# Chunked scan and two MoE layers on one core: fewer filler products, another order of weight-conversion steps before MoE1, and one scan request a chunk sooner

## The chip, the cores and the metric

The kernel runs on one core of a Trainium2 chip. The metric is device time in microseconds (us) of one execution. The five engines are named as in the profile: PE (TensorE, with PEld for its weight loads), DVE (VectorE), ACT (ScalarE), POOL (GpSimd) and SP (SyncE, which here only issues DMAs; the profile writes SPq for it).

## What is computed

A chunked state-space scan feeds two dense layers. Shortened from the reference:

```
# x [4,8,768,32], a [4,8,768], B and C [4,8,768,16]
la  = log(clip(a, 1e-6, 1));  cum = cumsum(la) inside a chunk
L   = exp(cum_i - cum_j), causal
y   = ((C B^T) * L) x  +  (C state) * exp(cum)
state = exp(sum la) * state + sum_j B_j x_j exp(cum_last - cum_j)
# y becomes x [3072, 256]
MoE1: h = x @ w_in;  g = max(h,0) + alpha*min(h,0);  x = g @ w_out     # d_ff 2048
MoE2: x = (sigmoid(x @ w_gate) * (x @ w_val)) @ w_out2                 # d_ff 1536
```

## The kernel before, in words

**Scan.** The four sequences of 768 positions are cut into 32 chunks of 96, eight to a sequence. A chunk c passes through four stages, each a function of its own. `ev_decay` (L367) multiplies the operands dl and dr into d on PE and has ACT take exp of it (L399), which gives lt. `ev_scores` (L403) multiplies B and C (tiles bt and ct) into cb on PE (L424). `ev_weigh` (L440) has DVE multiply cb by lt into mt (L448) and, for the first chunks, form bd (L459). `ev_out` (L461) multiplies on PE into yd (L472, L478), after which ACT copies the state to the next chunk's xs (L489) and the result to x1 (L491, or L484 for chunk 5). From chunk 7 on d has a single bank of PSUM, so the product of chunk c+1 waits until ACT's exp of chunk c has read it; cb has one bank from the start, so the scores of chunk c+1 wait for mt of chunk c.

**The loop (L1034).** Iteration i issues mt of chunk i (for early i), d of chunk i+1, yd of chunk i-1 and cb of chunk i+1, in that order on PE. For i below `lead` = 7 nothing else is there for PE, and `keep_busy` (L904) issues filler products of a constant tile (nobody<-heat, 128x512 bf16), whose result nobody reads: one at i = 0, three at i = 1 and 2, two at i = 3 to 6. From i = 7 on, one MoE1 step runs in each iteration: `moe1_in` (L520) multiplies the first 512 positions by a block of w_in into h, ACT forms t (L534), DVE forms g (L538), `halves` splits g into gh (ACT, L562) and gl (DVE, L563), and one iteration later `moe1_out` (L576) multiplies both by w_out into acc (L586). Before that, the finished chunks are split into xh (ACT L516, DVE L518), in three pieces.

**Weight conversion.** The weights come as 64-bit numbers. POOL requests them in tiles raw of 512 KB (L148), and `work` (L164) turns each into a high part and a low part in seven steps: 0 scale (ACT L160), 1 shift (DVE L190 or two of L193), 2 copy of the group before (L177: on POOL while i < 7, then on ACT), 3 clip (DVE L198), 4 low part of the group before (L179: on POOL while i < 7, then on DVE), 5 combine (DVE L202; for the first groups it also scales the next one on ACT), 6 combine (DVE L207). `feed(n, ...)` (L216) issues the next n steps. How many are issued in an iteration is `now` (L1078): EARLY = 4 for i = 1 to 6, then FIRST = 5 for the first eight MoE1 steps, then LATER = 4.

**Requests.** In each iteration SP requests dl and dr of chunk i+3 (`load_cum`, L322), xs of chunk i+3 (`load_x`, L278) and, once per four chunks, the bt and ct of a whole chunk group (`load_bc`, L292: one transfer of 192 KB for bt, four of 48 KB for ct, after dl, dr and xs of the same iteration). SP's transfers use eight counters in turn. A transfer is issued only when the one eight places ahead of it in SP's order, which has the same counter, has landed. Which chunk group is requested when is set by `soon` (L1072): the third group (chunks 8 to 11) at i = 5.

All engines work through their instructions in the order in which the program issues them, so the order of the calls in the loop is the order of the queues.

Of the kernel before, what the change touches and what calls it, by code (L numbers as in the profile page):

```python
# [37 lines left out]
AT_CHUNK = {1: 3, 4: 4, 5: 5, 6: 6, 7: 7}  # L38


EARLY = 4
FIRST = 5
LATER = 4

NX = 6
# [7 lines left out]
def kernel(  # L53
# [100 lines left out]
    def scale(g):  # L154

        if g < len(queue) and g not in mags:
            mags[g] = ring.tile([128, 2, WG], F32, tag="mag", name="mag", bufs=3)
            nc.scalar.activation(  # L160
                mags[g], raws[g][:, :, :, 1].bitcast(F32), AF.Copy, scale=2.0 ** -112
            )
# [53 lines left out]
    def feed(n, groups):  # L216

        for _ in range(n):
            if worked[0] < ready(groups - 1):
                work()  # L220
# [8 lines left out]
    first2 = len(queue)  # L229
# [18 lines left out]
    ZC = ZG * G  # L248
# [73 lines left out]
    def load_cum(c):  # L322
        b, k = divmod(c, CPB)
        s = slice(k * T, (k + 1) * T)
        if c < CPB - 1:

            rows = bf(parts[0:2 * H, s])
            for l in range(2):
                nc.sync.dma_start(out=bf(dr[c % NC][W + l:W + l + 1]), in_=rows[l:2 * H:2])
            nc.sync.dma_start(out=bf(dl[c % NC][T:W, 0:T]), in_=rows)  # L330
            return
        nc.sync.dma_start(
            out=bf(dl[c % NC][T:W, 0:T]), in_=cum_d[b].rearrange("h l s -> (h l) s")[:, s]
        )
        nc.sync.dma_start(
            out=bf(dr[c % NC][W:KD]), in_=cum_d[b, :, :, s].rearrange("h l t -> l h t")
        )
# [23 lines left out]
    lead = -(-BL // T) + 1  # L361
# [78 lines left out]
    def ev_weigh(c):  # L440
        MT[c] = m = aring.tile([W, H, T], F32, tag="mt", name="mt", bufs=3)
        last = ahead_of_this(nc.vector)
        if c >= ZC:
            split = lambda t: t.rearrange("j (q e) t -> j q (e t)", e=2)
            nc.vector.tensor_tensor(split(m), CBT.pop(c), split(LT[c]), op=ALU.mult)
        else:
            split = "j (e q) t -> j e q t" if c < ND else "j (q e) t -> j e q t"
            nc.vector.tensor_tensor(  # L448
                m.rearrange(split, e=2),
                CBT.pop(c)[:, :, 0:4 * T].rearrange("j e (q t) -> j e q t", t=T),  # L450
                LT[c].rearrange(split, e=2), op=ALU.mult,
            )
        if c % CPB < CPB - 1:
            BD[c] = bd = aring.tile([W, H, N], F32, tag="bd", name="bd", bufs=3)
            args = (bd, b_of(c), LT[c][:, :, T - 1:T].broadcast_to([W, H, N]))
            if c >= lead:
                behind(nc.gpsimd.tensor_tensor(*args, op=ALU.mult), last)
            else:
                nc.vector.tensor_tensor(*args, op=ALU.mult)  # L459
# [42 lines left out]
    def setup_flip():  # L502
        nc.vector.tensor_scalar(
            flip, sign.bitcast(U32), 0x80000000, None, op0=ALU.bitwise_and
        )
# [3 lines left out]
    def split_x(kind, k, lo=0, hi=BL, which="hl"):  # L509

        if lo == 0:
            xh[kind, k] = ring.tile([128, 2, KT, BL], F32R, tag="xs", name="xh", bufs=2)
        t = xh[kind, k][:, :, :, lo:hi]
        src = x1[:, :, k * BL + lo:k * BL + hi]
        if "h" in which:
            nc.scalar.copy(t[:, 0], src)  # L516
        if "l" in which:
            nc.vector.tensor_tensor(t[:, 1], src, bf(t[:, 0]), op=ALU.subtract)  # L518
# [50 lines left out]
    half = NF1 // 2  # L569
# [309 lines left out]
    with tc.manual_schedule():  # L879
# [24 lines left out]
        def keep_busy(n):  # L904
            p = psum.tile([128, 512], F32, tag="h", name="nobody")
            for _ in range(n):
                nc.tensor.matmul(p, heat[:, 0:128], heat, start=True, stop=True)  # L907
# [15 lines left out]
        def copy_eye(i):  # L923
            nc.gpsimd.tensor_copy(
                xs[i][T:W, H * D:].rearrange("s (h n) -> s h n", n=N),
                eye_c.unsqueeze(1).broadcast_to([N, H, N]),
            )
# [62 lines left out]
        def setup_left(j):  # L990

            nc.scalar.copy(dl[j][0:T], left_c)
            nc.scalar.copy(dl[j][T:KD], rows_c)

        def setup_right(j):
            (nc.vector.tensor_copy if j < 2 else nc.scalar.copy)(dr[j][0:W], bf(early_r))

        def follow(c):

            t = bf(dr[2]) if c == 0 else (MT if c == 1 else LT)[c]  # L1000
            nc.gpsimd.tensor_copy(scrap, t[0:1, 0, 0:1])
# [21 lines left out]
        def later_cum():  # L1023
            halve_cum(pieces[2], nc.scalar)
            for j in (2, 3):
                copy_eye(j)
            setup_alpha()
            store_cum()
# [4 lines left out]
        at = 0  # L1033
        for i in range(NCH + 1):  # L1034
            go = i >= lead
            early[0] = not go
            if i < min(NCH, ZC):
                ev_weigh(i)

            if i == lead // 2 + 1:  # L1040
                split_x("m1", 0, 0, BL // 2)
            if i == lead - 1:
                split_x("m1", 0, BL // 2, (lead - 2) * T)
            if i == 0:
                later_cum()
            if i == 1:
                setup_left(1)
                load_cum(4)
                scale(0)
                for j in range(2):  # L1050
                    setup_right(j)
                keep_busy(2)
            if i == lead:
                for h in range(2):
                    nc.gpsimd.dma_start(
                        out=units_z[h:128:2],
                        in_=k_misc[64 * h:64 * h + 64, 0:N].rearrange("(n k) c -> k n c", k=NP),
                    )
            if i in AT_CHUNK:
                follow(i)  # L1060
                ahead[0] = AT_CHUNK[i]
                take_up()
            if i == 1:
                for j in range(4, NX):
                    copy_eye(j)
            if i == 2:
                setup_flip()
            if 1 < i < NCH - 3:
                load_cum(i + 3)
            if 1 < i < NCH - 3:  # L1070
                load_x(i + 3)
            soon = i + 3 + (i + 4 >= ZC)  # L1072
            if G < soon < NCH and soon % G == 0:
                load_bc(soon)
            if i == NCH:
                open_banks()
            over = at > 1 and ends[steps[at - 2][1:]][1]
            now = 0 if i == 0 else EARLY if not go else FIRST if at < half else LATER  # L1078
            if i >= ZC:
                high_half(steps[at - 1])  # L1080
                if over:
                    moe1_done(steps[at - 2][1], alone=True)
                    now = 1
                elif at - 1 in (half + 1, 2 * half + 1):
                    now = 5
                if i + 1 < NCH:
                    ev_decay(i + 1)
                feed(now, first2)
                now = 0
                low_half(steps[at - 1])  # L1090
            else:
                if at > 0:
                    halves(steps[at - 1])
                if over:
                    moe1_done(steps[at - 2][1])
                ev_decay(i + 1)
                if go:
                    feed(now // 2, first2)
                    now -= now // 2

            def chunk():
                if i + 1 == ZC:
                    open_banks()
                if i + 1 < NCH:
                    ev_scores(i + 1)
                ev_out(i - 1)
                if i + 1 < NCH:
                    ev_weigh(i + 1)

            if go:  # L1110
                step_in(at, "h", later=chunk if i + 1 >= ZC else None)
            if i + 1 < ZC:
                if i > 0:
                    ev_out(i - 1)
                ev_scores(i + 1)
            if not go:
                keep_busy(1 if i == 0 else 3 if i < 3 else 2)
            if go:
                if at > 0:
                    step_out(at - 1, two=False)  # L1120
                splits(at)
                at += 1
            if i == lead - 1:
                feed(1, first2)
                split_x("m1", 0, (lead - 2) * T, BL, "l")
                now -= 1
            feed(now, first2)

            if i in (10, 12):
                lo = (i - 10) * BL // 4  # L1130
                split_x("m1", 1, lo, lo + BL // 2)
# [132 lines left out]
```

## Time and profile before

| | before |
|---|---|
| median of 3 runs | 626.7 us (626.63 to 629.47) |
| the profiled execution | 627.08 us |
| its span | 625.2 us |
| PE busy | 618.9 us, 99% |
| DVE busy | 515.3 us, 82% |
| ACT busy | 364.5 us, 58% |
| POOL busy | 73.8 us, 12% |
| chain of work that ended last | PE 97%, ACT 1%, DVE 1% |

Busy time of PE is to be read with care: its products are pipelined and their ends are modelled. All times in the rows are us from the start of the span unless ns is written. The first 29 us are the scan alone, up to the first product of MoE1; from there to about 140 us scan and MoE1 run side by side; then come the rest of MoE1 and MoE2.

### The profile page before, as it was taken

The numbers are of one execution on the slowest core, as the hardware profiler recorded it, in microseconds if no ns is written. First come the engines' busy times: TensorE is split into PE (matmuls) and PEld (weight loads), VectorE is DVE, ScalarE is ACT, GpSimd is POOL, SyncE is SP. The second block draws the span as 40 slices with busy tenths as digits, with TensorE's granted clock in tenths as the row PEclk, the third lists the DMA queues.
The fourth block names the chain that finished last, engine by engine and source line by source line (L and its number), as shares of the span: only waits on it lengthen the run. The fifth ranks groups of instructions, "written<-read, shape, count | busy, mean of one in ns | idle before, by whom it ended". The sixth has DMA issues, their size and how long they took to land.

```text
span 625.2 us, 11455 instructions
## 1 busy us (share of the span) xinstructions
PE 618.9 (99%) x4430; PEld 519.2 (83%) x4430; DVE 515.3 (82%) x883; ACT 364.5 (58%) x725; POOL 73.8 (12%) x110
## 2 busy tenths in 40 slices
PE   9999999999999999999999999999999999999997
PEld 4466777778888888888888889999999999999996
DVE  7999988867878778787676988888888888888876
ACT  7988788875656665665565444544544544544443
POOL 9845211100000000000000000000000000000000
PEclk9999999999999999999999999999999999999999
DMA  6764534310121221210000000100100100100001
GB/s 203 223 185 123 168 118 125 119 35 17 53 68 35 68 68 37 65 35 0 2 0 1 1 1 1 35 1 1 35 1 1 35 2 1 35 2 1 34 1 35
DMA packets 19176, 30.73 MB, mean 49 GB/s; under 512 B 7226, under 2 KB 14562, under 8 KB 19122
## 3 DMA queue, kind: packets, MB, share of 16 engines
q0 software_dynamic: 5296, 18.45, 9.4%
q1 hardware_dynamic: 13314, 11.08, 6.1%
q8 instruction: 35, 0.57, 0.4%
q10 hardware_dynamic: 512, 0.47, 0.2%
q14 instruction: 19, 0.16, 0.1%
HBM read 26.58 MB, written 3.34 MB: 48 GB/s over the span
## 4 chain that ended last, share of the span: by engine, by line
PE 97%; ACT 1%; DVE 1%; issue 0%; DMA 0%; SPq 0%; ACTq 0%; DVEq 0%
PE acc L586 22%; PE h L529 21%; PE pb L725 10%; PE po L667 10%; PE pc L725 7%; PE pa L725 7%; PE po L672 5%; PE gate L617 3%; PE val L617 3%; PE cb L424 2%; PE yd L478 2%; PE nobody L907 1%; PE four L411 1%; PE four L374 1%; PE yd L472 1%; PE d L385 1%
## 5 line engine op out<-in xcount | busy, mean ns | idle before, releaser
L529 PE MATMUL h<-xh,win 128*128 128x512 f32 x576 | 147.1, 391 | 0.0
L529 PEld LDWEIGHTS h<-xh,win 128*128 128x128 f32 x576 | 106.8, 188 | 21.5 <-issue 0.2
L586 PE MATMUL acc<-gh,wout 128*128 128x512 f32 x384 | 105.8, 397 | 0.0
L538 DVE SCALAR_TENSOR_TENSOR g<-h,salpha,t 128x512 f32<-128x512 f32 x96 | 71.7, 747 | 18.8 <-ACT t L534 18.1
L586 PEld LDWEIGHTS acc<-gh,wout 128*128 128x128 f32 x384 | 70.1, 188 | 19.8 <-ACT t L534 3.3
L534 ACT ACTIVATE t<-h,sign 128x512 f32<-128x512 f32 x96 | 66.0, 688 | 32.5 <-PE h L529 31.8
L563 DVE TENSOR_TENSOR gl<-g,gh 128x512 fp32r<-128x512 f32 x79 | 54.3, 688 | 21.6 <-ACT gh L562 21.3
L562 ACT CAST gh<-g 128x512 fp32r<-128x512 f32 x79 | 49.0, 621 | 38.7 <-DVE g L538 38.7
L837 ACT ACTIVATE s<-cs 128x512 f32<-128x512 f32 x30 | 19.0, 633 | 86.7 <-DVE cs L836 86.7
L667 PE MATMUL po<-w2out,gh 128*128 128x512 f32 x240 | 65.3, 393 | 0.0
L586 PE MATMUL acc<-gl,wout 128*128 128x512 f32 x192 | 59.2, 390 | 0.0
L563 DVE TENSOR_TENSOR gl<-p,gh 128x512 fp32r<-128x512 f32 (+1 forms) x67 | 45.5, 679 | 12.4 <-ACT gh L562 12.4
L562 ACT CAST gh<-p 128x512 fp32r<-128x512 f32 (+1 forms) x72 | 44.3, 616 | 17.7 <-DVE p L864 9.7
L667 PEld LDWEIGHTS po<-w2out,gh 128*128 128x128 f32 x240 | 41.8, 190 | 6.1
L725 PE MATMUL pa<-xh,w2in 128*128 128x256 f32 x300 | 44.0, 282 | 0.0
L563 POOL TENSOR_TENSOR gl<-p,gh 128x512 fp32r<-128x512 f32 x5 | 6.5, 1297 | 308.4 <-PE pa L725 308.4
L586 PEld LDWEIGHTS acc<-gl,wout 128*128 128x128 f32 x192 | 36.0, 188 | 7.7
L672 PEld LDWEIGHTS po<-w2out,gl 128*128 128x128 f32 x240 | 36.3, 188 | 5.7 <-POOL gl L563 1.1
L725 PEld LDWEIGHTS pa<-xh,w2in 128*128 128x128 f32 x300 | 39.3, 190 | 0.0
L672 PE MATMUL po<-w2out,gl 128*128 128x256 f32 x240 | 38.3, 281 | 0.0
L836 DVE TENSOR_TENSOR cs<-pb,cs 128x512 f32<-128x512 f32 x30 | 20.7, 690 | 15.5 <-PE pb L725 15.5
L160 ACT ACTIVATE mag<-raw 128x512 f32<-128x512 f32 x34 | 22.6, 668 | 12.9 <-DVE w2in L179 7.1
(190 smaller groups left out, 1115.7 us busy)
## 6 DMA issues: line engine op xcount, KB each, us to landing
raw<-in_moe_w_out_dram POOLq DMA_DIRECT2D x14, 512.0 KB, 4.0
xs<-in_xb_dram SPq DMA_DIRECT2D x32, 144.0 KB
raw<-in_moe_w_in_dram POOLq DMA_DIRECT2D x8, 512.0 KB, 4.6
raw<-in_moe_w_gate_dram POOLq DMA_DIRECT2D x6, 512.0 KB, 4.1
raw<-in_moe_w_val_dram POOLq DMA_DIRECT2D x6, 512.0 KB, 4.1
out_dram<-osb SPq DMA_DIRECT2D x10, 256.0 KB
bt<-in_bc_dram SPq DMA_DIRECT2D x32, 24.0 KB
ct<-in_bc_dram SPq DMA_DIRECT2D x8, 96.0 KB
```

What stands on the lines that cost most here:

```text
L160: nc.scalar.activation(mags[g], raws[g][:, :, :, 1].bitcast(F32), AF.Copy, scale=2.0 ** -112)
L529: nc.tensor.matmul(h, w[:, wl, kt, :], xh["m1", k][:, xl, kt, :], start=(i == 0 and kt == 0), stop=(i == 2 and kt == KT - 1),)
L534: nc.scalar.activation(t, h, AF.Identity, scale=sign[:, f:f + 1])
L538: nc.vector.scalar_tensor_tensor(g, h, salpha[:, f:f + 1], t, op0=ALU.mult, op1=ALU.max)
L562: nc.scalar.copy(gh[:, cs], g[:, cs])
L563: e.tensor_tensor(gl[:, cs], g[:, cs], bf(gh[:, cs]), op=ALU.subtract)
L586: nc.tensor.matmul(acc[k][:, m], w[:, wl, m * 128:(m + 1) * 128], g, start=(first and i == 0), stop=(last and i == 2),)
L617: nc.tensor.matmul(p, w[:, wl, kt, :], xh["m2", k][:, xl, kt, :], start=(i == 0 and kt == 0), stop=(i == 2 and kt == KT - 1),)
L667: nc.tensor.matmul(o[e][:, u].rearrange("p (l d) -> p l d", l=2), ph[:, ts], w, start=(f == 0), stop=False, skip_group_check=True,)
L672: nc.tensor.matmul(o[e][:, u, 0:DM], pl[:, ts], w[:, 0, :], start=False, stop=last, skip_group_check=True,)
L725: nc.tensor.matmul(bank[:, e], left_of(e, j, a, wl), right_of(k, b, xl), start=first and e == i == 0, stop=i == 2, skip_group_check=True,)
L836: tt(cs[:, :, 0], b, cs[:, :, 0], op=ALU.add)
```

## The change

Four places differ. The number of filler products falls from three to two at i = 1 and 2 and from two to one at i = 3 to 6. The number of conversion steps per iteration changes from 4, 4, 4, 4, 4, 4 for i = 1 to 6 to 4, 4, 4, 2, 5, 2, and from 5, 5 to 7, 6 for the first two MoE1 steps, after which both have issued 34. At i = 6 both steps now come ahead of the last split of xh on DVE. And `load_bc` of the third chunk group is called at i = 4 instead of i = 5.

```
-EARLY = 4
-FIRST = 5
+EARLY = {0: 0, 4: 2, 5: 5, 6: 2}
+FIRST = {0: 7, 1: 6}
...
-            soon = i + 3 + (i + 4 >= ZC)
+            soon = i + (4 if i < lead or i + 4 >= ZC else 3)
...
-            now = 0 if i == 0 else EARLY if not go else FIRST if at < half else LATER
+            now = EARLY.get(i, 4) if not go else FIRST.get(at, 5) if at < half else LATER
...
-                keep_busy(1 if i == 0 else 3 if i < 3 else 2)
+                keep_busy(2 if 0 < i < 3 else 1)
...
             if i == lead - 1:
-                feed(1, first2)
+                feed(now, first2)
                 split_x("m1", 0, (lead - 2) * T, BL, "l")
-                now -= 1
+                now = 0
             feed(now, first2)
```

What the numbers do to the queues shows in the order of the instructions. On ACT, around iterations 5 to 8 (xs_107 and xs_102 are the states of chunks 5 and 6, xs_103 that of chunk 7; L160 is a scale step, L399 an exp, L177 a copy step, L534 the t of the first MoE1 step):

```order
 L489 COPY xs_107<-yd 16x2x32 x4
 L491 COPY x_76<-yd 128x2x96
-L160 ACTIVATE mag<-raw 128x512
 L516 CAST xh<-x_76 128x2x224
 L399 ACTIVATE lt<-d 112x768
...
 L516 CAST xh<-x_76 128x2x32
 L489 COPY xs_102<-yd 16x2x32 x4
-L399 ACTIVATE lt<-d 112x768
+L160 ACTIVATE mag<-raw 128x512
+L399 ACTIVATE lt<-d 112x768
+L177 CAST win_77<-mag 128x512
 L534 ACTIVATE t<-h,sign 128x512
```

One scale step moved from ahead of the exp of chunk 7 (the first L399 shown) to ahead of the exp of chunk 8 (the second), and a copy step that POOL had now stands on ACT ahead of the first t.

On DVE, from iteration 4 to the first MoE1 step (the three L448 are mt of chunks 5, 6 and 7; L538 is the first g):

```order
 L207 SCALAR_TENSOR_TENSOR mag<-mag,raw 128x512
-L190 TENSOR_SCALAR raw<-raw 128x512
 L448 TENSOR_TENSOR mt<-cb,lt 112x2x4x96
 L459 TENSOR_TENSOR bd<-xs_107,lt 112x128
...
+L448 TENSOR_TENSOR mt<-cb,lt 112x2x4x96
 L193 TENSOR_SCALAR raw<-raw,flip 128x256 x2
-L448 TENSOR_TENSOR mt<-cb,lt 112x2x4x96
+L538 SCALAR_TENSOR_TENSOR g<-h,salpha,t 128x512
 L198 TENSOR_SCALAR mag<-mag 128x512
 L179 TENSOR_TENSOR win_77<-mag,win_77 128x512
-L538 SCALAR_TENSOR_TENSOR g<-h,salpha,t 128x512
```

A shift step (L190) no longer stands ahead of mt of chunk 5, mt of chunk 7 now stands ahead of two shift steps, and the first g stands ahead of a clip and a low-part step (L198, L179) where it stood behind them.

On SP, in the changed kernel, from the requests of iteration 4 on (dl_109, dr_112 and xs_103 belong to chunk 7; bt_114 and ct_116 to the third chunk group; dl_110, dr_113 and xs_104 to chunk 8; dl_108 to chunk 9; in brackets the counters that each waits for):

```order
L332 DMA dl_109<-cum_d 16x96 [waits DMAHW1_49,DMASW2_49,PE_49]
L335 DMA dr_112<-cum_d 2x8x96 [waits DMAHW2_49]
L282 DMA xs_103<-in_xb_dram 96x384 [waits DMAHW3_49,DVE_49]
L314 DMA bt_114<-in_bc_dram 128x4x96 [waits DMAHW4_49]
L320 DMA ct_116<-in_bc_dram 32x384 [waits DMAHW5_49]
L320 DMA ct_116<-in_bc_dram 32x384 [waits DMAHW6_49]
L320 DMA ct_116<-in_bc_dram 32x384 [waits DMAHW7_49]
L320 DMA ct_116<-in_bc_dram 32x384 [waits DMAHW0_49]
L332 DMA dl_110<-cum_d 16x96 [waits DMAHW1_49,PE_49]
L335 DMA dr_113<-cum_d 2x8x96 [waits DMAHW2_49]
L282 DMA xs_104<-in_xb_dram 96x384 [waits DMAHW3_49,DVE_49]
L332 DMA dl_108<-cum_d 16x96 [waits DMAHW4_49,PE_49]
```

Before, the five transfers of bt_114 and ct_116 stood behind dl, dr and xs of chunk 8 and ahead of dl of chunk 9.

## Rows read from the trace of the kernel before

**Rows 1.** The page: busy time, share of the span and instructions of each engine.

```profile
PE 618.9 (99%) x4430; PEld 519.2 (83%) x4430; DVE 515.3 (82%) x883; ACT 364.5 (58%) x725; POOL 73.8 (12%) x110
```

**Rows 2.** Windows: stretch, length, busy us (instructions) by engine, clock, DMA share, GB/s.

```profile
15.00:20.00 5.00, 5.00 (x84) 2.54 (x82) 4.96 (x11) 4.37 (x14) 4.44 (x9) 1.00 0.57 153
...
35.00:60.00 25.00, 25.00 (x257) 16.58 (x256) 23.86 (x41) 20.95 (x52) 12.65 (x12) 1.00 0.48 146
...
300.00:600.00 300.00, 300.00 (x1995) 276.14 (x1994) 250.89 (x434) 142.78 (x272) 6.49 (x5) 1.00 0.03 10
```

**Rows 3.** Timeline of PE: start, length, line, tiles, count, idle time before and its releaser.

```profile
1.46 4.88 PE L907 MATMUL nobody<-heat 128*128 128x512 bf16 x11 [1.46 <-DVE heat L902]
...
15.05 0.82 PE L907 MATMUL nobody<-heat 128*128 128x512 bf16 x3
...
20.07 0.60 PE L907 MATMUL nobody<-heat 128*128 128x512 bf16 x2
...
24.79 0.90 PE L424 MATMUL cb<-ct,bt 64*112 64x384 f32 x4 [0.62 <-DVE mt L448]
...
28.32 0.60 PE L385 MATMUL d<-dr,dl 114*112 114x384 f32 x2
28.85 1.63 PE L529 MATMUL h<-xh,win 128*128 128x512 f32 x6
...
31.53 0.90 PE L424 MATMUL cb<-ct,bt 64*112 64x384 f32 x4 [0.49 <-DMA dr<-cum_d]
...
34.74 0.90 PE L424 MATMUL cb<-ct,bt 64*112 64x384 f32 x4
```

**Rows 4.** Timeline of ACT, 25 to 35 us.

```profile
25.59 0.32 ACT L491 COPY x<-yd 128x192 f32<-128x192 f32 x1
26.40 0.70 ACT L160 ACTIVATE mag<-raw 128x512 f32<-128x512 f32 x1 [0.49 <-DMA raw<-in_moe_w_out_dram]
27.00 0.56 ACT L516 CAST xh<-x 128x448 fp32r<-128x448 f32 x1
27.45 0.81 ACT L399 ACTIVATE lt<-d 112x768 f32<-112x768 f32 x1
...
29.65 0.81 ACT L399 ACTIVATE lt<-d 112x768 f32<-112x768 f32 x1
30.51 0.69 ACT L534 ACTIVATE t<-h,sign 128x512 f32<-128x512 f32 x1
...
34.64 0.64 ACT L177 CAST wout<-mag 128x512 fp32r<-128x512 f32 x1
```

**Rows 5.** Timeline of DVE, 23 to 35 us.

```profile
23.45 0.43 DVE L190 TENSOR_SCALAR raw<-raw 128x512 uint32<-128x512 uint32 x1
23.79 0.94 DVE L448 TENSOR_TENSOR mt<-cb,lt 112x768 f32<-112x768 f32 x1
...
28.93 0.98 DVE L193 TENSOR_SCALAR raw<-raw,flip 128x256 uint32<-128x256 uint32 x2
...
30.69 0.41 DVE L198 TENSOR_SCALAR mag<-mag 128x512 f32<-128x512 f32 x1
...
31.63 0.74 DVE L538 SCALAR_TENSOR_TENSOR g<-h,salpha,t 128x512 f32<-128x512 f32 x1
...
33.61 0.95 DVE L448 TENSOR_TENSOR mt<-cb,lt 112x768 f32<-112x768 f32 x1
```

**Rows 6.** Timeline of SP's queue: start and length of each issue, 23 to 30 us.

```profile
23.52 0.41 SPq L314 DMA_DIRECT2D bt<-in_bc_dram  x1
23.98 3.23 SPq L320 DMA_DIRECT2D ct<-in_bc_dram  x4
...
26.12 1.09 SPq L320 DMA_DIRECT2D ct<-in_bc_dram  x1
...
27.31 0.66 SPq L332 DMA_DIRECT2D dl<-cum_d  x1
...
29.48 0.33 SPq L282 DMA_DIRECT2D xs<-in_xb_dram  x1
```

## The prediction

> **What bounds the kernel now.** The first view is the page's busy time: PE is busy for 618.9 of 625.2 us [rows 1], so the reader looks for the places where PE is not supplied. The windows show where these cannot be: from 35 to 60 us PE is busy for 25.00 of 25.00 us and from 300 to 600 us for 300.00 of 300.00, all at a granted clock of 1.00 [rows 2]. From 35 us on nothing can be caught up and nothing is lost, so whatever the change moves before 35 us stays in the end time as it is. All edits lie before that. The next view is therefore the timeline of the first 35 us, engine by engine. Its end is a product that both kernels share, cb of chunk 9 at 34.74 [rows 3], behind which PE runs without a gap. The question is by how much that start moves. On PE two waits show ahead of it: cb of chunk 6 waits 0.62 us for mt of chunk 5, cb of chunk 8 waits 0.49 us for a transfer [rows 3]. ACT stands idle for 0.49 us before a scale step, which waits for the weights, with the exp of chunk 7 behind it [rows 4]. On DVE no row between 28.93 and the end of mt of chunk 8 at 34.56 shows a wait [rows 5]: there DVE is full, and cb of chunk 9 starts 0.18 us after that mt. So DVE, not PE, holds the place that decides.
>
> **Fillers.** Six go. Three take 0.82 us and two 0.60 [rows 3], so one costs 0.22 and six 1.3 us of PE. I book nothing. Their cover is DVE, busy for 4.96 of 5.00 us from 15 to 20, and ACT with 4.37 [rows 2]: PE reaches its next product sooner and waits for mt or lt. If PE were what the chunks wait for, the gain would be the whole 1.3; the other bound is a loss by the clock, below.
>
> **Chunk 5 on DVE.** The shift step at 23.45 no longer precedes mt of chunk 5 at 23.79 [rows 5]: 0.34 us less, out of the 0.62 that cb of chunk 6 waits. It helps d of chunk 7 to be there in time for the next item, and has no price of its own.
>
> **The scale step on ACT.** The copy of chunk 4 ends at 25.91 and the split (L516) starts at 27.00 [rows 4]: with the wait and the scale step gone, 1.09 us less. The exp of chunk 7 starts at 26.36 instead of 27.45 and ends at 27.17. Before, d of chunk 8 started at 28.32, right after that exp [rows 3, 4], since d has one bank. It could now start at 27.2, and the first MoE1 product, 0.53 behind it, at 27.7 instead of 28.85.
>
> **What returns on ACT.** The same scale step (0.70) now stands ahead of the exp of chunk 8, and the copy step, which POOL did, stands on ACT ahead of t (0.64, from the same operation at 34.64) [rows 4]. The exp starts at 29.65 - 1.09 + 0.70 = 29.26; t starts 0.86 later, as before (30.51 - 29.65), plus 0.64, that is at 30.76, and ends at 31.45 (before: 31.20). ACT has taken back what it gave.
>
> **The first g on DVE.** Now L538 stands ahead of the clip and the low-part step. Before, these two ran while t was still being made; the time from the clip to g is 31.63 - 30.69 = 0.94, and from g to mt of chunk 8 it is 33.61 - 31.63 = 1.98 [rows 5]. After, g starts when t is there, 31.48 at the earliest, and 0.94 + 1.98 = 2.92 follow: mt of chunk 8 at 34.40 instead of 33.61. It takes 0.95 and cb of chunk 9 starts 0.06 later: 35.41, that is +0.67. Before g, DVE will stand idle, for mt of chunk 7 and the two shift steps are done by then. This holds even when every transfer is in time.
>
> **The request one chunk sooner.** The gain: cb of chunk 8 no longer waits 0.49 [rows 3]. The price: on SP five transfers (384 KB) now stand ahead of dl, dr and xs of chunk 8. When these land follows from who waits for the eighth before it. The fourth ct was issued at 26.12, when xs of chunk 7 had landed; dl of chunk 9 at 27.31, so dl of chunk 8 had landed within 1.2 us of that; xs of chunk 9 at 29.48, when xs of chunk 8 had landed [rows 6]. The five had landed when cb of chunk 8 started, at 31.53 [rows 3], 2.05 after xs of chunk 8. In the new order they follow xs of chunk 7: 26.12 + 2.05 = 28.17, and dl and dr behind them, half of their 1.2 us: 28.8. Then d of chunk 8, ready on ACT's side at 27.2, waits for dr until 28.8, and the first MoE1 product waits behind it on PE. The bounds: not late at all (27.2), or late by shares of bytes. All from xs of chunk 7 to the five took 31.53 - 26.12 = 5.41 us for 540 KB, and 396 KB now come ahead: 26.12 + 3.97 = 30.1. I take 28.8, between them, as it rests on the row of the five transfers themselves.
>
> The trace has no view in which a small transfer passes a large one of its queue. The Trainium skill (DMA: Bandwidth & Descriptors, section "Two DMAs through the same engine are not ordered") says that descriptors of one queue on one engine start in order: by that dl and dr can't start ahead of the five, and the sum below stands; if they overtook, it would be the 0.67 above.
>
> **Sum.** From d of chunk 8 to cb of chunk 9: 0.53 to the first MoE1 product, 1.63 for it, 0.69 for t, 0.03, 2.92 on DVE, 0.95 + 0.06 for mt: 6.81 us [rows 3 to 5]. From 28.8 that gives 35.6 against 34.74: **+0.9 us**. Before, the same path took 34.74 - 28.32 = 6.42, which is why the change needs d of chunk 8 at 27.9 to break even. Late transfers (30.1) give 36.9: +2.2. The three steps left out before MoE1 cost nothing more: both orders have issued 34 after the second MoE1 step. On the profiled execution's 627.08 us the sum makes 628.0; that one lies 0.4 above the median of the runs, 626.7, which becomes **627.6**.
>
> **Rivals.**
>
> *It pays.* PE leads and DVE follows: the first MoE1 product moves by 1.1, and the 0.49 at cb of chunk 8 goes too, -1.6: 625.1 us. For it: both waits are in the rows. Against it: ACT's t is late by its own queue, and DVE has nothing to give up. It needs dr of chunk 8 by 27.2 and a g that isn't waited for. Chance: 0.20.
>
> *Nothing is left.* One of the two prices is half as large, or the fillers' 0.2 per chunk does reach d: within 0.4 us of 626.7. Chance: 0.20.
>
> *The transfers are later than I take them.* The DMA queues carry weights at the same time; dr of chunk 8 lands at 30.1 or after: +2.2 and somewhat more, 628.9. Chance: 0.15.
>
> *The clock falls (slower).* With fewer fillers and a wait of about 2 us ahead of d of chunk 8, PE is emptier than at any place since the start. The first eleven fillers took 4.88 us, 0.44 each, against 0.22 later [rows 3]: 1.2 GHz there, 2.4 GHz after. If the clock drops in this wait and comes back only at cb of chunk 9, the work from d of chunk 8 to there, 34.74 - 28.32 - 0.49 = 5.9 us, takes twice as long: +0.9 + 5.9, 633.5 us. It decides from about 2.2 us of work at the lower level. Against it: the clock stays at 1.00 in all the windows, also where PE had waited [rows 2]. The Trainium skill (TensorE: Matmul & The Clock Gate, section "What's actually happening") has it that "the default state is throttled, and activity releases the throttle", which speaks against taking fillers out; by it alone the time is that 633.5. Chance: 0.04.
>
> **How the numbers follow.** The forecast, a loss of 0.4 to 1.7 us, has 0.40; with the rivals that is 0.99, and 0.01 is for a gain of over 3 us, which no row offers. About 0.5%, 3.1 us, is what a measurement of this kernel can tell from no change. The forecast and the first three rivals lie within it: 0.95; to the slower side belong the clock and the far end of late transfers, 0.03; to the faster 0.02. The range takes in the gain of 1.6 and the late transfers: 625.1 to 629.1, where about one in ten is left out on account of the clock and of two mishaps at once.
>
> **What would show it.** Right: d of chunk 8 starts later than 28.3 although the exp of chunk 7 ends at about 27.2; a row of idle time ahead of the first L538 on DVE, ended by ACT's t; no wait at cb of chunk 8; cb of chunk 9 at 35.4 to 36; then no idle time on PE that was not there before, so that the end is later by the same amount. Wrong: d of chunk 8 before 27.9, or a first g that DVE does not have to wait for; a cb of chunk 9 at 33 to 34; a clock under 1.00; waits on PE at the second or third MoE1 step, which would mean that the moved conversion steps come too late for w_out.

## The result and the profile after

| | before | after |
|---|---|---|
| median of 11 runs, in turns on one chip | 627.8 us (626.63 to 630.21) | 630.9 us (629.3 to 632.66) |
| ratio, 95% interval | | 1.0053 [1.004, 1.0066] |
| the profiled execution, its span | 627.08, 625.2 us | 631.26, 629.2 us |

The change costs 3.3 us (2.5 to 4.1; a ratio here rests on all runs and is not the quotient of the two medians). The prediction had the sign of its sum, +0.9, but not its size: 630.9 lies above its range. A part of the distance is the kernel before itself, which came out at 627.8 and not at the 626.7 from which the prediction counted; but the 3.1 us between the two medians also lie beyond the +2.4 that its range left.

The page of the changed kernel opens with the line that answers to [rows 1]:

```profile
PE 617.5 (98%) x4424; PEld 518.6 (82%) x4424; DVE 515.0 (82%) x883; ACT 365.1 (58%) x726; POOL 73.2 (12%) x109
```

Six products fewer, 1.4 us less on PE, and a span 4.0 us longer: PE waits. The timeline of PE in the changed kernel, from the last filler to h of the third MoE1 step (start, length, line, product; in brackets idle time ahead of it and what ended it):

```profile
28.23 0.39 PE L907 MATMUL nobody<-heat 128*128 128x512 bf16 x1
31.73 0.57 PE L385 MATMUL d<-dr,dl 114*112 114x384 f32 x2 [3.11 <-DMA dl<-cum_d]
32.14 1.56 PE L529 MATMUL h<-xh,win 128*128 128x512 f32 x6
...
34.20 0.90 PE L424 MATMUL cb<-ct,bt 64*112 64x384 f32 x4
35.03 0.60 PE L385 MATMUL d<-dr,dl 114*112 114x384 f32 x2
35.48 1.55 PE L529 MATMUL h<-xh,win 128*128 128x512 f32 x6
...
38.40 0.90 PE L424 MATMUL cb<-ct,bt 64*112 64x384 f32 x4 [0.90 <-DVE mt L448]
...
41.07 1.30 PE L529 MATMUL h<-xh,win 128*128 128x512 f32 x5
```

Against [rows 3]: d of chunk 8 at 31.73 instead of 28.32, cb of chunk 9 at 38.40 instead of 34.74, +3.66. The next h starts at 41.07; before, at 37.42, so +3.65, and that is carried to the end. The wait of 0.49 us at cb of chunk 8 is gone, and a wait of 3.11 us for dl of chunk 8 stands ahead of it, at d. SP's queue, against [rows 6]:

```profile
22.14 0.43 SPq L314 DMA_DIRECT2D bt<-in_bc_dram  x1
22.61 2.45 SPq L320 DMA_DIRECT2D ct<-in_bc_dram  x4
25.16 0.53 SPq L332 DMA_DIRECT2D dl<-cum_d  x1
...
27.73 0.24 SPq L335 DMA_DIRECT2D dr<-cum_d  x1
29.24 0.32 SPq L282 DMA_DIRECT2D xs<-in_xb_dram  x1
30.63 0.30 SPq L332 DMA_DIRECT2D dl<-cum_d  x1
31.43 0.24 SPq L335 DMA_DIRECT2D dr<-cum_d  x1
```

dl of chunk 8 was asked for at 25.16 and let d go at 31.73: 6.6 us for 6 KB. The last four rows (dr and xs of chunk 9, dl and dr of chunk 10) each stand eight places behind one of the four ct and waited for it, so the ct landed at about 27.7, 29.2, 30.6 and 31.4. dl was there 0.3 us behind the last of them. Before, dl of chunk 8 was asked for 2.8 us sooner:

```profile
22.36 0.36 SPq L332 DMA_DIRECT2D dl<-cum_d  x1
```

ACT and DVE of the changed kernel have the order that the prediction built on ([rows 4, 5]):

```profile
26.46 0.32 ACT L491 COPY x<-yd 128x192 f32<-128x192 f32 x1
...
27.28 0.80 ACT L399 ACTIVATE lt<-d 112x768 f32<-112x768 f32 x1
...
33.10 0.61 ACT L177 CAST win<-mag 128x512 fp32r<-128x512 f32 x1
33.74 0.69 ACT L534 ACTIVATE t<-h,sign 128x512 f32<-128x512 f32 x1
```

```profile
34.46 0.75 DVE L538 SCALAR_TENSOR_TENSOR g<-h,salpha,t 128x512 f32<-128x512 f32 x1 [3.54 <-ACT t L534]
35.12 0.42 DVE L198 TENSOR_SCALAR mag<-mag 128x512 f32<-128x512 f32 x1
...
37.39 0.95 DVE L448 TENSOR_TENSOR mt<-cb,lt 112x768 f32<-112x768 f32 x1
```

The exp of chunk 7 starts at 27.28, only 0.17 us sooner than before, because the copy of chunk 4 ahead of it came 0.87 us later (26.46 against 25.59). The copy step stands ahead of t, DVE waits for the first g, and from that g to mt of chunk 8 it takes 37.39 - 34.46 = 2.93 us; the prediction had 2.92.

### The profile page after: what moved, and what is told of

The parts are those of the page before. It is cut to its first block, busy times and chain, and to the rows that moved or that the text cites. A ratio compares the mean times of both kernels' runs of the same rounds, so it can differ in the third digit from the quotient of the medians.

```text
span 629.2 us, 11445 instructions
## 1 busy us (share of the span) xinstructions
PE 617.5 (98%) x4424; PEld 518.6 (82%) x4424; DVE 515.0 (82%) x883; ACT 365.1 (58%) x726; POOL 73.2 (12%) x109
## 4 chain that ended last, share of the span: by engine, by line
PE 93%; DMA 3%; DVE 2%; SPq 1%; ACT 0%; issue 0%; ACTq 0%; DVEq 0%
PE acc L586 22%; PE h L529 21%; PE pb L725 10%; PE po L667 10%; PE pc L725 7%; PE pa L725 7%; PE po L672 5%; PE gate L617 3%; PE val L617 3%; PE yd L478 1%; PE four L411 1%; PE cb L424 1%; DMA dl<-cum_d 1%; PE four L374 1%; PE yd L472 1%; DMA xs<-in_xb_dram 1%
## 5 line engine op out<-in xcount | busy, mean ns | idle before, releaser
L538 DVE SCALAR_TENSOR_TENSOR g<-h,salpha,t 128x512 f32<-128x512 f32 x96 | 71.8, 748 | 22.5 <-ACT t L534 21.9
L534 ACT ACTIVATE t<-h,sign 128x512 f32<-128x512 f32 x96 | 66.0, 688 | 33.0 <-PE h L529 32.3
L160 ACT ACTIVATE mag<-raw 128x512 f32<-128x512 f32 x34 | 22.6, 665 | 12.2 <-DVE w2in L179 6.9
```

The lines of the kernel that those rows point to most:

```text
L160: nc.scalar.activation(mags[g], raws[g][:, :, :, 1].bitcast(F32), AF.Copy, scale=2.0 ** -112)
L534: nc.scalar.activation(t, h, AF.Identity, scale=sign[:, f:f + 1])
L538: nc.vector.scalar_tensor_tensor(g, h, salpha[:, f:f + 1], t, op0=ALU.mult, op1=ALU.max)
```

## Experiments

Each kernel ran in five rounds in turns with the kernel before; "before" is the median of that chip. Two questions stood: is it the request or the conversion order, and what makes the request so dear?

**One part at a time.** The request alone is the `soon` line of the change put into the kernel before; the second kernel is the changed one with that line put back; the third has only the numbers of the conversion order; the fourth only the fillers:

```
request_alone:     +soon = i + (4 if i < lead or i + 4 >= ZC else 3)      # in the kernel before
request_back:      +soon = i + 3 + (i + 4 >= ZC)                          # in the changed kernel
conversion_alone:  +EARLY, FIRST, now, feed(now), now = 0 of the change   # in the kernel before
fillers_alone:     +keep_busy(2 if 0 < i < 3 else 1)                      # in the kernel before
```

> The kernel before with only the request of B and C of chunk group 2 one chunk sooner. Theory Q (the small transfers dl and dr of chunk 8 land late behind the five, and that wait is the whole loss): d of chunk 8 waits on PE for dl or dr until 31 to 32 us, cb of chunk 9 starts 6.4 us after it (the old path length) at about 37.6 to 38.4, and the time is +2.5 to +3.6 us. Rival V (the conversion order is what costs, by the first g that DVE waits for): d of chunk 8 waits little, and the time is -0.5 to +0.8 us.

> The changed kernel with the request of B and C put back to where it was; fillers and conversion order stay changed. Theory Q: d of chunk 8 starts at 27 to 28 us without a wait for dl or dr; what is left is the first g on DVE: -0.5 to +0.7 us against the kernel before. Rival V: the first L538 on DVE still waits over 3 us for t, and the time is +2 to +3.5 us.

> The kernel before with the new conversion order alone (all fillers, the old request). Theory Q: within -0.5 and +0.9 us of before; the first g starts when t is there, 31.0 to 31.5 us, and cb of chunk 9 at 34.5 to 35.4. Rival V: +2 to +3.5 us. If the fillers are worth something of their own, this one is slower than the changed kernel with the old request, by up to 1.3 us.

> The kernel before with the fewer fillers alone. Theory N (DVE and ACT cover them): within -0.4 and +0.4 us. Rival: the 1.3 us of PE are worth something, -0.5 to -1.3 us; or the clock falls more often without them, with runs of a mean clock under 0.998 and a median above +0.5 us.

| | median | before | ratio, 95% interval |
|---|---|---|---|
| request_alone | 630.27 | 627.07 | 1.0041 [1.0029, 1.0054] |
| request_back | 628.11 | 627.07 | 1.0023 [1.0012, 1.0034] |
| conversion_alone | 628.24 | 627.07 | 1.0017 [1.0008, 1.0026] |
| fillers_alone | 627.12 | 626.8 | 1.0005 [0.9997, 1.0014] |

The fillers are worth nothing that can be measured. The conversion order costs 1.1 us (0.5 to 1.6), the request by itself 2.6 (1.8 to 3.4). Three of the five runs of request_alone had a mean clock of 0.997 and took 630.27 to 630.5 us; the two at 1.0 took 628.87 and 628.97, 1.8 to 1.9 us above before. request_back came out above the +0.7 that theory Q allowed it. On DVE conversion_alone shows why it costs, without any late transfer:

```profile
32.13 0.75 DVE L538 SCALAR_TENSOR_TENSOR g<-h,salpha,t 128x512 f32<-128x512 f32 x1 [1.15 <-ACT t L534]
...
35.06 0.96 DVE L448 TENSOR_TENSOR mt<-cb,lt 112x768 f32<-112x768 f32 x1
```

DVE stands idle for 1.15 us ahead of g and then needs 2.93 to mt of chunk 8; before, it was 1.98 and no idle time [rows 5]. request_alone has the old conversion order, and d of chunk 8 waits all the same, somewhat less long than the 31 to 32 us expected:

```profile
30.71 0.57 PE L385 MATMUL d<-dr,dl 114*112 114x384 f32 x2 [1.75 <-DMA dl<-cum_d]
```

**What makes dl late.** Three kernels take the same changed order and ease the request in different ways: dl and dr ahead of the five transfers; only bt sooner; one weight transfer of POOL's queue a chunk later (AT_CHUNK lists the iterations at which POOL asks for the next weights).

```
small_first:    load_cum(8), load_bc(8) right behind ev_decay(5), in iteration 4; load_x(8) as it was
half_ahead:     bt of chunk group 2 at i = 4, its four ct at i = 5, behind load_x(8)
weights_later: -AT_CHUNK = {1: 3, 4: 4, 5: 5, 6: 6, 7: 7}
               +AT_CHUNK = {1: 3, 4: 4, 6: 6, 7: 7}
```

> The changed kernel, but dl and dr of chunk 8 are requested ahead of the five transfers of B and C, which stand right behind them, with xs of chunk 8 behind. The same bytes move, B and C still about a chunk sooner than before. Theory Q: dl and dr land by 27.2, d of chunk 8 starts at 27 to 28 without such a wait, cb of chunk 8 does not wait for a transfer, and the time is -1 to +0.4 us against before. Rival V: +2 to +3.5 us. Rival B (not the order but the bytes: the five take bandwidth from everything else): dl and dr are in time but xs or the weights are late, and the time is +1 to +3 us.

> The changed kernel with half of the bytes ahead of dl and dr of chunk 8: bt (192 KB) one chunk sooner, the four ct (192 KB) at the old place. Theory Q by bytes: d of chunk 8 starts half way between 27.3 (none ahead) and 31.7 (all), at 29 to 30, and the time is +1.5 to +2.6 us against before. Rival L (it is the many small rows of ct that are slow): d of chunk 8 by 28 and +0.9 to +1.5 us. Rival A (any large transfer ahead costs the whole): 31 or later, +2.8 to +3.6 us.

> The changed kernel with one of the weight transfers (512 KB on POOL's queue, issued at 23.7 us) requested one chunk later, at about 27.5, together with the next; nothing else moves. Theory S (the small transfers are late because the weights on the other queue share the engines with the five ahead of them): dl of chunk 8 lands 1 to 2 us sooner, d of chunk 8 at 29.7 to 30.8, the time +1.3 to +2.7 us, unless ACT or DVE then wait for that weight group. Rival O (own queue alone): d of chunk 8 at 31.4 or later, +2.8 to +3.6 us.

| | median | before | ratio, 95% interval | d of chunk 8 |
|---|---|---|---|---|
| small_first | 628.33 | 627.07 | 1.0021 [1.0012, 1.0029] | 27.52 |
| half_ahead | 628.22 | 627.07 | 1.0019 [1.0008, 1.0031] | 27.53 |
| weights_later | 628.3 | 627.07 | 1.0022 [1.0009, 1.0034] | 27.86 |

In all three d of chunk 8 is there in time, and all three stand near conversion_alone, 1.2 to 1.4 us above before; for small_first that is more than the +0.4 that Q allowed. So Q by bytes falls with half_ahead (not half the wait but none), and S gave a smaller effect than there is. Rival L, the small rows of ct, forecast both figures of half_ahead and is not excluded as a part of the cause: no run put the ct alone ahead of dl. In weights_later the ct stand ahead of dl, too, and d does not wait, so they are not enough by themselves.

weights_later leaves SP's order as the change has it, five transfers ahead of dl, and only POOL's requests move. d of chunk 8 and POOL's rows there, from the weights' request ahead of the five on:

```profile
27.86 0.57 PE L385 MATMUL d<-dr,dl 114*112 114x384 f32 x2
```

```profile
21.18 0.76 POOL L148 DMA_DIRECT2D raw<-in_moe_w_out_dram  x1
...
26.61 0.74 POOL L148 DMA_DIRECT2D raw<-in_moe_w_in_dram  x1
27.35 0.72 POOL L148 DMA_DIRECT2D raw<-in_moe_w_out_dram  x1
```

In the changed kernel these were at 22.10, 23.66 and 27.51. One transfer of 512 KB moved by 3 us, and dl, on the other queue, lands at least 3.9 us sooner (27.86 against 31.73), although it was asked for as late as in the changed kernel (25.27 against 25.16). So it is neither the order on SP nor the later request by itself that makes dl late, nor the bytes ahead alone, but these together with the weights. What the two queues moved from the request of bt to the start of d of chunk 8 shows it (kind, packets, MB, share of 16 engines; q0 carries POOL's transfers, q1 SP's): first the changed kernel (22.14 to 31.73), then the same kernel in a second profile, changed_again (22.62 to 31.41), then weights_later (21.71 to 27.86):

```profile
q0 software_dynamic: 474, 1.55, 48.5%
q1 hardware_dynamic: 1210, 0.87, 33.0%
...
q0 software_dynamic: 554, 1.84, 61.1%
q1 hardware_dynamic: 981, 0.64, 26.3%
...
q1 hardware_dynamic: 1008, 0.67, 39.5%
q0 software_dynamic: 144, 0.52, 22.8%
```

SP's queue moved 0.64 to 0.87 MB in each; the weights' queue moved three times as much where dl was late, though these stretches are also longer (9.6 and 8.8 us against 6.2). In the changed kernel's stretch a packet of the weights' queue is 1.55 MB / 474 = 3.3 KB, one of SP's 0.72 KB. The Trainium skill (DMA: Bandwidth & Descriptors, section "Queues, rings and completion order") says that an engine takes the queues in turn, packet by packet, where a packet is a group of descriptors and need not be what the profile counts. An estimate from that rule and these two sizes is that the weights get some four and a half times the bytes of SP's queue while both have work. Over the two stretches it was 1.8 and 2.9 times; no run here shows the turns themselves.

**The clock.** Of the 11 runs of the changed kernel, five had a mean granted clock of 0.999 and a median of 630.1 us, six had 0.995 to 0.997 and 632.2. To fill the wait without moving a transfer, nine fillers were put into it; later the changed kernel and this one ran side by side.

```
-keep_busy(2 if 0 < i < 3 else 1)
+keep_busy(10 if i == 6 else 2 if 0 < i < 3 else 1)
```

> The changed kernel with nine fillers more (ten instead of one) ahead of d of chunk 8, some 2 us of products inside the wait of 3.1 us. Theory C (of the changed kernel's loss a part is the clock, which falls in that wait in some executions: five of its eleven runs had a mean clock of 0.999 and a median of 630.1 us, six had 0.995 to 0.997 and 632.2): now no run is under 0.998, the spread goes and the median is +2.0 to +2.7 us against before. Rival W (the wait for dl alone, the clock as a bystander): the same two groups as before, +2.9 to +3.6 us. If the fillers themselves delayed anything, it would be slower than +3.6.

> The changed kernel itself once more, beside the next one on the same chip. Theory C (wait and clock): again two groups, mean clock 0.998 and over at about +2.3 us, 0.997 and under at +3.5 to +5 us, median between. Rival W (wait alone): one group, +2.9 to +3.5 us, whatever the clock.

> The changed kernel with ten fillers instead of one ahead of d of chunk 8, as once before. Theory C: no run under 0.998, and the median 0.3 to 1.2 us below that of the changed kernel on the same chip. Rival W: the same median within 0.2 us.

| | median (range) | before | ratio, 95% interval | runs with a clock of 0.997 or less |
|---|---|---|---|---|
| fillers_in_the_wait | 629.56 (629.44 to 629.82) | 626.8 | 1.0045 [1.0033, 1.0057] | 0 of 5 |
| changed_again | 631.53 (630.0 to 632.72) | 627.0 | 1.0066 [1.0052, 1.008] | 5 of 6 |
| fillers_in_the_wait_again | 629.74 (629.53 to 630.84) | 627.0 | 1.0046 [1.0034, 1.0058] | 0 of 5 |

The profile of changed_again caught the fall. Its PE:

```profile
31.41 0.95 PE L385 MATMUL d<-dr,dl 114*112 114x384 f32 x2 [3.58 <-DMA dl<-cum_d]
32.16 2.76 PE L529 MATMUL h<-xh,win 128*128 128x512 f32 x6
...
35.84 1.42 PE L424 MATMUL cb<-ct,bt 64*112 64x384 f32 x4
...
39.62 0.90 PE L424 MATMUL cb<-ct,bt 64*112 64x384 f32 x4
```

and its windows (stretch, length, busy us of PE, PEld, DVE, ACT, POOL, granted clock, DMA share, GB/s):

```profile
28.00:30.00 2.00, 0.00 (x0) 0.00 (x0) 2.00 (x5) 1.28 (x4) 1.53 (x3) 1.00 0.94 302
30.00:31.00 1.00, 0.00 (x0) 0.00 (x0) 0.09 (x1) 0.00 (x0) 0.00 (x0) 0.55 0.77 227
...
34.00:36.00 2.00, 2.00 (x37) 1.07 (x37) 0.32 (x1) 0.71 (x2) 0.00 (x0) 0.50 0.31 90
36.00:37.00 1.00, 1.00 (x4) 0.29 (x4) 1.00 (x3) 0.95 (x5) 0.00 (x0) 0.54 0.00 0
37.00:38.00 1.00, 1.00 (x6) 0.77 (x5) 0.97 (x2) 1.00 (x3) 0.00 (x0) 1.00 0.05 16
```

PE did nothing for 3.58 us, the clock fell to 0.50 (1.2 GHz) at about 30 us, and just under seven us later it was back. The same six products h took 2.76 us instead of 1.56, and from d to cb of chunk 8 it is 35.84 - 31.41 = 4.43 us, against 34.20 - 31.73 = 2.47 at the full clock: 1.96 us. At cb of chunk 9, which waits for mt of chunk 8 on DVE (done at 39.56), 1.54 of them are left: 39.62 - 31.41 = 8.21 instead of 6.67. With fillers in the wait no run of ten lost its clock, and the median on the same chip is 1.8 us lower, more than the 0.3 to 1.2 expected. Not all of this need be the clock: when dl lands differs between executions, and in the two profiles with fillers it landed sooner. The one run of changed_again at a clock of 0.999 took 630.2 us, 0.5 above the median with fillers. That kernel still waits for its transfer (d of chunk 8 at 29.85 and 30.07 in its profiles) and still loses 2.8 us, so the wait and the conversion order are the larger part.

**A version that keeps the gain?** Five kernels tried to take back the price on DVE, two of them with weights_later as well; a sixth puts small_first into the kernel before.

```
clip_ahead_of_g:        small_first, and feed(5) ahead of step_in at at == 0, 2 steps behind it
clip_ahead_all_fillers: the same with keep_busy as before
steps_behind_mt:        small_first, and FIRST = {0: 5, 1: 8}
behind_mt_weights_later: the changed kernel with weights_later and FIRST = {0: 5, 1: 8}
behind_mt_weights_later_small_first: steps_behind_mt with weights_later
small_first_on_before:  the kernel before with small_first's requests
```

> The small requests first (as in that run), and on DVE the clip and the low-part step (L198, L179) ahead of the first L538 again; nothing else moves. Theory G (the rest of the loss, +1.3 us, is the 2.92 us on DVE between the first t and mt of chunk 8): the 1.14 us in which DVE waited for t is used, mt of chunk 8 starts at about 33.3 instead of 34.2, cb of chunk 9 at 34.3 instead of 35.25, and the time is +0.1 to +0.6 us against before. Rival P (PE or ACT would hold cb of chunk 9 there anyway): +1.0 to +1.6 us, with cb of chunk 9 at 35 or later.

> As clip_ahead_of_g, with the fillers of the kernel before. Theory C (two of that kernel's twelve runs, 630.4 and 631.5, had a mean clock of 0.997 and had lost it where fillers are missing): no run above +1.6, median -0.3 to +0.7 us against before. Rival: fillers have nothing to do with it, and one or two runs in ten again lie 3 to 4 us above the median.

> The small requests first, and of the seven conversion steps of the first MoE1 step two ahead of it and three behind, the other two moved to the second step: the copy (L177) stands behind t on ACT, L202 and L207 behind mt of chunk 8 on DVE. Theory G: t of the first step starts at about 30.1, g at 30.8, mt of chunk 8 at 32.5, cb of chunk 9 at 33.6 to 34.0; the time is -0.6 to +0.3 us against before. Rival D (DVE is full, so two steps put off come back at the next item): cb of chunk 9 early, but cb of chunk 10 or h of the third step late, +0.5 to +1.4 us.

> A version put together from the parts: the changed kernel with one weight transfer later (as in weights_later) and the conversion steps of the first MoE1 step behind t and mt (as in steps_behind_mt). Theory (nothing late on SP, and no 2.92 us ahead of mt of chunk 8): d of chunk 8 at 27.9, d of chunk 9 at 31 without a wait, cb of chunk 9 at 33.4 to 34.2, and the time -0.9 to -0.1 us against before. Rival D (DVE is full and takes it back at the next item, or the weight group comes late): +0.3 to +1.2 us.

> The same with dl and dr of chunk 8 ahead of the five as well. Theory: d of chunk 8 at 27.3 instead of 27.9; -1.2 to -0.1 us against before. Rival D: +0.3 to +1.2 us, or d of chunk 9 waits for its own dl behind the five.

> The kernel before, its conversion order and all its fillers, with the request one chunk sooner but dl and dr of chunk 8 ahead of it. The wait of 0.49 us at cb of chunk 8 goes. Theory D (DVE, full from 28.9 to 34.6, holds cb of chunk 9): cb of chunk 9 within 0.3 of where it was relative to d of chunk 8, and the time -0.3 to +0.3 us. Rival E (the early request does pay once nothing is late): -0.5 to -0.9 us.

| | median | before | ratio, 95% interval |
|---|---|---|---|
| clip_ahead_of_g | 627.56 | 626.8 | 1.0024 [1.0011, 1.0037] |
| clip_ahead_all_fillers | 627.7 | 627.07 | 1.001 [1.0001, 1.0019] |
| steps_behind_mt | 627.43 | 626.8 | 1.0008 [0.9999, 1.0016] |
| behind_mt_weights_later | 628.31 | 627.0 | 1.0026 [1.0012, 1.004] |
| behind_mt_weights_later_small_first | 627.83 | 627.0 | 1.0028 [1.001, 1.0047] |
| small_first_on_before | 627.48 | 627.07 | 1.0005 [0.9996, 1.0013] |

None beats the kernel before. Where the clip and the low-part step stand ahead of g again, the median falls from 1.3 to 0.8 us above before (0.6 with all fillers), which is still more than theory G's +0.6. The ratio of clip_ahead_of_g, 1.0024, lies higher, since two of its twelve runs lost their clock (630.42 and 631.49 at 0.997). DVE of clip_ahead_of_g:

```profile
30.44 0.69 DVE L179 TENSOR_TENSOR win<-mag,win 128x512 fp32r<-128x512 f32 x1 [0.22 <-ACT win L177]
31.04 0.75 DVE L538 SCALAR_TENSOR_TENSOR g<-h,salpha,t 128x512 f32<-128x512 f32 x1
...
33.04 0.95 DVE L448 TENSOR_TENSOR mt<-cb,lt 112x768 f32<-112x768 f32 x1
```

The idle time ahead of g is gone and mt of chunk 8 starts 1.2 us sooner than in small_first (34.24), 0.3 of it because d of chunk 8 did. So the rows make the order on DVE a part of the conversion order's price; its size, some 0.5 us, is not shown, since it comes from medians of different chips and the intervals overlap. steps_behind_mt is the nearest to before of the five, but came out above the +0.3 expected: its profile has d of chunk 9 waiting 1.59 us instead. The row names a copy on ACT, but of ACT that product needs only the exp of chunk 8, done at 30.41; what else it needs are its dl and dr, which now stand behind the five and xs of chunk 8. SP's xs of chunk 11, eight places behind that dl, waited for it until 32.33. The two combined versions did not get the gain expected of them: in the profile of the first, d of chunk 8 waits 0.51 us and d of chunk 9 1.41 us for dr, and three and five of their runs had a clock of 0.997 or less. In small_first_on_before cb of chunk 8 waits for nothing and cb of chunk 9 starts sooner than before, and then PE shows:

```profile
34.17 0.90 PE L424 MATMUL cb<-ct,bt 64*112 64x384 f32 x4
...
37.70 1.67 PE L529 MATMUL h<-xh,win 128*128 128x512 f32 x6 [0.53 <-DVE g L538]
```

cb of chunk 9 came at 34.17 instead of 34.74, but the next h at 37.70 instead of 37.42: PE, ahead by 0.57, waits for g, and the 0.49 us that the early request was to win are given back one item later. Theory D put that down to a full DVE. The rows name something else: DVE itself stands idle for 0.97 and 0.78 us there, for gh and t of ACT, and ACT had waited for weights:

```profile
33.87 0.68 ACT L160 ACTIVATE mag<-raw 128x512 f32<-128x512 f32 x1 [0.96 <-DMA raw<-in_moe_w_out_dram]
```

So t of that step starts at 36.16 instead of 35.15. Two more profiles in which cb of chunk 9 comes sooner show the same wait: fillers_alone (cb at 33.81, a wait of 1.01) and behind_mt_weights_later_small_first (34.34, 1.10). What these weights would be worth if they were asked for sooner was not tried.

## Why the prediction missed

**Right:** that PE's waits ahead of 35 us decide and a loss there is carried to the end (+3.66 at cb of chunk 9, +3.65 at the next h, +4.0 in the spans). That the fillers are worth nothing (1.0005). That the exp of chunk 7 is freed of the scale step and ACT takes the step back ahead of t, though this exp started at 27.28 and not at 26.36. That g now waits for t and 2.92 us follow to mt of chunk 8 (measured 2.93 in three profiles), and that this has a price with every transfer in time: 0.67 forecast, 1.1 (0.5 to 1.6) in conversion_alone. That the wait at cb of chunk 8 moves to d of chunk 8. And the path from there: 6.81 predicted, 38.40 - 31.73 = 6.67 in the profile.

**Wrong, the step that failed:** the time at which the five transfers, and dl and dr behind them, land: "26.12 + 2.05 = 28.17, and dl and dr behind them, half of their 1.2 us: 28.8." The order was right, the size was not: the last ct landed at about 31.4, and d of chunk 8 started at 31.73 and 31.41 in the two profiles of the changed kernel, beyond even the bound of 30.1. Put 31.73 into the prediction's own sum and it gives 31.73 + 6.81 - 34.74 = +3.8 us, where the two spans differ by 4.0. The 2.05 us that were taken for the five transfers were read from a stretch (29.48 to 31.53) at whose start they had been requested for 3.4 to 6.0 us already [rows 6]: what was measured was their tail. Counted from the request of bt, the five took up to 8.0 us before (23.52 to 31.53) and 9.3 in the changed kernel (22.14 to 31.43). And the bound by shares counted only the bytes of SP's own queue; weights_later shows that 512 KB on POOL's queue decide whether dl lands by 27.9 or at 31.7. The prediction named the weights, in the rival that the transfers come later, but priced it at "+2.2 and somewhat more".

**A reading that carried little:** "DVE, not PE, holds the place that decides." In the kernel before, PE has no idle time ahead of cb of chunk 9:

```profile
34.27 0.54 PE L478 MATMUL yd<-mt,xs 112*32 112x96 f32 x16
```

mt of chunk 8 was done at 34.56, and 0.06 behind it, as at cb of chunk 6, cb could have started at 34.62; it started at 34.74. PE held it by 0.12 us, with DVE close behind.

**The clock rival** had a chance of 0.04 and a price of 5.9 us. In 11 of 17 runs of the changed kernel the mean clock was 0.997 or less, and the one profile of such a run shows the fall at this place. It cost a third of that price, since the clock came back before cb of chunk 9, and DVE, not PE, held what followed. The argument against it, that the clock stays at 1.00 where PE had waited, rested on waits of 0.62 us and less [rows 3], and no window of [rows 2] holds even one of them; here the wait was 3 us. The "1.2 GHz there" of the first eleven fillers was read from their length; the granted clock of that trace is 1.00 from 2 to 7 us. That the clock was taken as safe is a part of the miss: the changed kernel's runs at a mean clock of 0.999 were 2.3 us above before, the others 4.4.

**Open:** what the conversion order costs beyond cb of chunk 9. There, small_first, half_ahead and weights_later are only 0.4 to 0.5 us behind before (35.16 to 35.26 against 34.74), while they lose 1.2 to 1.4 in the end. With nothing late and the clip ahead of g, 0.6 to 0.8 us stay. Whether the copy on ACT ahead of t or the scale step ahead of the exp of chunk 8 holds them was not tried apart. And of the late dl it is open which part the small rows of ct have beside the weights.

## What to carry to other kernels

A transfer's duration can't be read from the time at which the next one lands: take the time of issue, and count all that is pending on every queue, not on one's own. Before a large request is moved ahead, list the small ones behind it and the first instruction that needs each; here 12 KB that were wanted at 27.5 outweighed the 0.49 us won. And where one engine gets ahead, ask what it meets next: here a gain shrank or was gone within an item, in three profiles beside a wait of about 1 us for weights on ACT, while a loss stayed.

## What the runs showed of the hardware

A wait for a transfer can cost twice. In request_alone PE stood idle for only 1.75 us ahead of d of chunk 8 (28.96 to 30.71), and its windows show the clock falling when the work was already back:

```profile
30.00:31.00 1.00, 0.29 (x2) 0.32 (x3) 1.00 (x3) 0.00 (x0) 1.00 (x2) 1.00 0.60 172
31.00:32.00 1.00, 1.00 (x6) 0.82 (x5) 0.56 (x1) 0.63 (x1) 1.00 (x4) 0.83 0.98 380
32.00:33.00 1.00, 1.00 (x4) 0.59 (x2) 0.00 (x0) 0.18 (x1) 0.63 (x1) 0.50 0.87 254
...
35.00:36.00 1.00, 1.00 (x7) 0.49 (x4) 0.96 (x2) 0.98 (x4) 0.00 (x0) 0.96 0.72 265
```

In the profile of the changed kernel the wait was longer, 3.11 us, and the clock stayed at 1.00:

```profile
30.00:32.00 2.00, 0.27 (x2) 0.30 (x3) 0.92 (x3) 0.13 (x1) 1.64 (x2) 1.00 0.76 250
32.00:34.00 2.00, 2.00 (x36) 1.46 (x38) 0.00 (x0) 1.58 (x3) 0.00 (x0) 1.00 0.81 243
```

So the changed kernel with its wait takes some 2 us more in some executions than in others (medians of 632.2 and 630.1 us), and a single profile doesn't tell which.

Clock losses were also commoner in the kernels with the fewer fillers and no long wait at d of chunk 8: 16 of 104 runs of nine kernels had a mean clock of 0.997 or less, against 2 of 147 runs of the kernels with all fillers (before, conversion_alone, small_first_on_before, clip_ahead_all_fillers). The eleven runs of the kernel before that stand beside the result are not among these; their clocks are not on record. That the fillers are the cause is not shown: fillers_alone and steps_behind_mt, which lack them too, had no such run in 22, and in the one profile that caught such a loss, of request_back, the clock is 0.50 from 11 us on, which lies ahead of the first place where a filler is missing.
